# Two cached attention blocks on one core: every tile as two half-width loads, one per DMA queue

## The chip, the cores and the metric

The kernel runs on one core of a Trainium2 chip. The metric is the device time of one execution in microseconds, lower is better.

## The reference

Two independent decode blocks, A and B, have the same shapes: 8 sequences, one new token each, width 1024, 32 heads of 128, and a cache of 4096 keys and values. All inputs are bf16.

```python
# for each of A and B
q = (x @ wq).reshape(8, 1, 32, 128).transpose(0, 2, 1, 3)
scores = einsum("bhqd,bhkd->bhqk", q, k_cache) * 128 ** -0.5
p = softmax(scores)
o = einsum("bhqk,bhkd->bhqd", p, v_cache)
out = o.transpose(0, 2, 1, 3).reshape(8, 1, 4096) @ wo
# and the two results side by side along the last axis
```

The two caches of a block hold 2 x 268 MB; with the four projection matrices the kernel reads 1107 MB, and every byte of it once.

## The kernel before, in words

The work is cut into 64 iterations (`NQ`), each for one block, one sequence and 8 heads. An iteration n has one K tile and one V tile. A tile is 128 partitions x 64 KB = 8.39 MB: partition (head, m) holds 256 consecutive positions of the cache, 64 KB that are contiguous in HBM too. The projection matrices `wq` and `wo` of the two blocks are tiles of the same size, so there are 132 tiles in all.

SBUF has room for three tiles, the `ring`. In the steady state K tiles alternate between slots 0 and 1, and every V tile goes to slot 2. The order is written out by hand in `plan`:

```python
plan = [("wq", 0, 1), ("k", 0, 0), ("wq", 1, 2)]
for n in range(NQ - 1):
    plan.append(("k", n + 1, (n + 1) % 2))
    plan.append(("v", n, 2))
plan += [("v", NQ - 1, NQ % 2), ("wo", 0, 2), ("wo", 1, (NQ - 1) % 2)]
```

`load_tiles` (L257) goes down this list and issues a load as soon as the operation that last uses the slot's previous tenant has been written into the program (`opUse`); the load then waits on a semaphore for that operation. For V(n) this is the second half of PV of n-1 (L382), for K(n+2) it is the last reduction matmul group of n (L345). In the kernel before, V loads are issued by ScalarE on its own DMA queue, all other tiles by SyncE. Each ring slot has one semaphore, and each `dma` call adds 16 to the count that its readers wait for. Output rows go out on both queues, and the two small x inputs come in on ScalarE's.

The program is a list of operations per engine, written in one order; each engine executes its own list in that order. An iteration has four chunks r = 0..3 of a K tile:

- DVE multiplies the chunk by the broadcast query (L330, in place), folds its halves (L335), and one chunk later sums what PE has reduced (L353).
- PE reduces the folded chunk by matmuls with the identity (`make_eacc`, L345). At r = 2 the first half of PV of iteration n-1 stands ahead of that reduction on PE, and so does the broadcast of the next query (L317); at r = 3 the second half of PV does (L382). `make_ext` (L399) follows after the reduction of r = 3.
- At r = 0 the softmax of n-1 is done: maximum (L359), exp on ScalarE (L365), and the spread probabilities `PM` on DVE (L370).
- ScalarE copies PV's result (L390, `make_acc`), the extracted output (L405) and stages and copies the next query (L312, L319).

At r = 3 the order of the writing is PV's second half, `make_acc`, the reduction, `load_tiles`, `make_ext`. So `load_tiles` there issues V(n) and K(n+2), in this order. PE's and DVE's lists are folded into hardware loops of two iterations; ScalarE's and SyncE's are straight code. After the loop the last softmax, the normalization (L418, L419) and the output projections (L433) follow. The last `wo` is loaded in three pieces (`wo_cuts`), of 48, 12 and 4 KB in each partition.

Of the kernel before, what the change touches and what calls it, by code (L numbers as in the profile page):

```python
# [31 lines left out]
class _Program:  # L32
# [11 lines left out]
    def add(self, eng, emit, deps=(), dma_key=None, moves=False):  # L44
        op = _Op(eng, emit, list(deps), dma_key, moves)
        if dma_key is not None:
            self.counts[dma_key] = self.counts.get(dma_key, 0) + 16
            op.token = (dma_key, self.counts[dma_key])
        for d in op.deps:
            if not (d.eng == "pe" and eng == "pe"):  # L50
                d.sig = True
        self.ops[eng].append(op)
        return op
# [86 lines left out]
def _build_kernel(nc, caches, out):  # L140
    B, Sq, D = caches[0][0].shape
    _, H, Sk, Dh = caches[0][1].shape
    NC = len(caches)
    assert B == 8 and Sq == 1 and Dh == 128 and Sk == 4096 and D == 1024 and H % 8 == 0 and 128 % H == 0
    DC = D // 128
# [16 lines left out]
    with es:  # L162
# [45 lines left out]
        def dma(out_ap, in_ap, key, deps, eng="sp"):  # L208
            return add(eng, lambda e: e.dma_start(out_ap, in_ap), deps, dma_key=key)


        def pool_select(view, base, pattern, dep, op=ALU.not_equal, fill=1.0, step=1):
            return add("pool", lambda e: e.affine_select(out=view, in_=view, compare_op=op, fill=fill,
                                                         base=base, pattern=pattern, channel_multiplier=step), [dep])
        c_ident = pool_select(ident[:], 0, [[-1, 128]], add("pool", lambda e: e.memset(ident[:], 0.0)))


        c_own = add("pool", lambda e: e.memset(own_m[:], 1.0))
        c_own = pool_select(own_m[:], 0, [[-MP, HQ], [0, PH]], c_own, ALU.is_ge, 0.0)
        c_own = pool_select(own_m[:], MP - 1, [[MP, HQ], [0, PH]], c_own, ALU.is_ge, 0.0, -1)  # L220
        own = own_m[:, :, 0]

# [8 lines left out]
        opT, opMul, opEacc, opRed, opNgm, opExp = {}, {}, {}, {}, {}, {}  # L231
# [18 lines left out]
        def where(n):  # L250

            return n // (B * HB), n // HB % B, n % HB
# [4 lines left out]
        def load_tiles():  # L257
            while issued[0] < len(plan):
                kind, n, w = plan[issued[0]]
                prev = before[issued[0]]  # L260
                dep = opUse.get(prev)
                if prev is not None and dep is None:
                    return
                to, key = ring[:, w, :], ("t", w)
                if kind in ("k", "v"):
                    c, b, hb = where(n)
                    from_ = caches[c][1 if kind == "k" else 2][b, hb * HQ:(hb + 1) * HQ].rearrange("u (m t) d -> (u m) (t d)", m=MP)
                    opT[(kind, n)] = dma(to, from_, key, [dep], "act" if kind == "v" else "sp")
                elif kind == "wq":
                    opT[(kind, n)] = dma(to[:, 0:DC * H * Dh], caches[n][3].rearrange("(p k) n -> p (k n)", k=DC), key, [dep])  # L270
                else:
                    from_ = caches[n][4].rearrange("(p r) n -> p (r n)", r=H)
                    for i, (r0, r1) in enumerate(wo_cuts if n == NC - 1 else ((0, H),)):
                        opT[(kind, n, i)] = dma(to[:, r0 * D:r1 * D], from_[:, r0 * D:r1 * D], key if n < NC - 1 else ("w", i), [dep])
                issued[0] += 1


# [169 lines left out]
        def emit_xT(e):  # L447
# [5 lines left out]
            return i  # L453
        op_xT = opUse[("x", 0)] = add("pe", emit_xT, [c_ident, op_x[-1]])
        load_tiles()
        c_xT = add("dve", lambda e: e.tensor_copy(xT[:], misc_bf16[:, 0:NC * DC * B]), [op_xT])
        make_q(0)
# [5 lines left out]
        for n in range(NQ):  # L463
            P.mark(n)
            for r in range(NR):
                s = n * NR + r
                make_mul(s)
                if s >= LAG:
                    make_red(s - LAG)
                if r == LAG - 1 and n >= 1:  # L470
                    make_shift(n - 1)
                fold = make_fold(s)
                if r == LAG - 1 and n >= 1:
                    make_pm(n - 1)
                if n == 0 and r == 1:
                    for c in range(1, NC):
                        make_q(c)
                        make_qT(c)
                if r == 2 and n >= 1:
                    make_pv(n - 1, 0, RG // 2)  # L480
                if r == 3 and n >= 1:
                    make_pv(n - 1, RG // 2, RG)
                    make_acc(n - 1)
                if r == 2 and n + 1 < NQ:
                    make_stage(n + 1)
                    make_qbc(n + 1)
                make_eacc(s, fold)
                load_tiles()
                if r == 3 and n >= 1:
                    make_ext(n - 1)  # L490
        P.mark(NQ)
        n = NQ - 1
# [4 lines left out]
        make_pv(n, 0, RG)  # L497
        make_acc(n)
        load_tiles()
        make_ext(n)  # L500
        make_norm(1)
# [31 lines left out]
def bass_concat_heads__mha_block_cached__mha_block_cached__decode_kernel(  # L533
    nc, A_x, A_k_cache, A_v_cache, A_wq, A_wo, B_x, B_k_cache, B_v_cache, B_wq, B_wo, out,
):
    caches = [(A_x, A_k_cache, A_v_cache, A_wq, A_wo), (B_x, B_k_cache, B_v_cache, B_wq, B_wo)]
    _build_kernel(nc, caches, out)
# [28 lines left out]
```

## Time and profile before

| | |
|---|---|
| median of 3 runs | 2931.91 us (2924.83 to 2936.99) |
| the profiled execution's own time | 2936.99 us |
| its span | 2935.2 us |
| DMA, mean over the span | 377 GB/s, 1107.53 MB |
| share of the two load queues (q1 SyncE, q10 ScalarE) | 44.9% and 43.7% of 16 engines |
| DVE, PE, ScalarE busy | 74%, 39%, 4% |
| TensorE clock granted | 0.688 of full speed |

The span runs from the first to the last instruction of the profiled execution. "Busy" is the time of the instructions themselves. In the chain of waits each moment is put down to what held up the end; a DMA in it counts from its issue to its landing. The line numbers L... are those of the kernel before.

### The profile page before, as it was taken

What the parts mean: (1) busy time and instruction counts of PE and PEld (TensorE: products, weight loads), DVE (VectorE), ACT (ScalarE), POOL (GpSimd) and SP (SyncE); (2) the same over time, 40 slices, a digit from 0 to 9 for tenths busy, and PEclk for the clock granted to TensorE, in tenths of its full rate; (3) what the DMA queues carried; (4) which work ended last, traced back from release to release, by engine and by line L of the source; (5) the groups of instructions that cost most, each with busy time, mean ns of one, the idle gap of its engine ahead of it and who ended that gap; (6) DMA issues with size and microseconds to landing.
All of it is one profiled execution on the core that took longest, in us unless ns stands there. A gap on an engine that the chain in (4) does not pass through costs nothing.

```text
span 2935.2 us, 18256 instructions
## 1 busy us (share of the span) xinstructions
PE 1155.4 (39%) x7648; PEld 401.4 (14%) x7648; DVE 2172.8 (74%) x1043; ACT 130.0 (4%) x401; POOL 2.5 (0%) x14
## 2 busy tenths in 40 slices
PE   2433443443433334334334434333344344344344
PEld 1111111111111111111111111111111111111112
DVE  2977768778778678777777787786777877877864
ACT  1000000000000000000000000000000000000000
POOL 0000000000000000000000000000000000000000
PEclk7666766766667667767767666676676676676667
DMA  9989889889889898898898898898988988988989
GB/s 428 401 371 388 372 343 400 372 372 400 357 372 400 343 400 372 359 400 370 372 400 343 372 398 359 372 400 343 400 351 364 400 371 358 400 372 372 395 348 387
DMA packets 19436, 1107.53 MB, mean 377 GB/s; under 512 B 2208, under 2 KB 2256, under 8 KB 2400
## 3 DMA queue, kind: packets, MB, share of 16 engines
q1 hardware_dynamic: 10128, 570.45, 44.9%
q10 hardware_dynamic: 9296, 536.92, 43.7%
q8 instruction: 7, 0.11, 0.0%
q14 instruction: 5, 0.04, 0.0%
HBM read 1107.33 MB, written 0.03 MB: 377 GB/s over the span
## 4 chain that ended last, share of the span: by engine, by line
DMA 79%; PE 17%; DVE 3%; another core or an unknown queue 0%; issue 0%; ACT 0%; SPq 0%; DVEq 0%
DMA ring<-in_A_v_cache_dram 39%; DMA ring<-in_B_v_cache_dram 37%; PE pv L382 11%; PE red L345 5%; DVE ring L330 1%; DMA ring<-in_A_k_cache_dram 1%; DMA ring<-in_B_wo_dram 1%; DVE ring L335 1%; PE misc L317 0%; DVE s_sb L353 0%; PE proj L433 0%; DVE PM L370 0%; PE o L285 0%; PE pv L285 0%
## 5 line engine op out<-in xcount | busy, mean ns | idle before, releaser
L330 DVE TENSOR_TENSOR ring<-ring,qbc 128x8192 bf16<-128x8192 bf16 x256 | 1131.4, 4420 | 13.6 <-DMA ring<-in_A_k_cache_dram 13.6
L345 PE MATMUL red<-ring,ident 128*128 128x512 bf16 x2048 | 746.2, 530 | 927.0 <-DVE ring L335 927.0
L353 DVE TENSOR_REDUCE s_sb<-red 128x64 f32<-128x1024 f32 x256 | 312.2, 1220 | 659.8 <-PE red L345 659.8
L382 PE MATMUL pv<-ring,PM 128*32 128x512 bf16 x4096 | 349.5, 502 | 799.9 <-DMA ring<-in_A_v_cache_dram 400.1
L335 DVE TENSOR_TENSOR ring<-ring 128x4096 bf16<-128x4096 bf16 x256 | 582.2, 2274 | 0.0
L345 PEld LDWEIGHTS red<-ring,ident 128*128 128x128 bf16 x2048 | 237.1, 125 | 1357.8 <-DVE ring L335 1023.8
L382 PEld LDWEIGHTS pv<-ring,PM 128*32 128x32 bf16 x4096 | 118.9, 117 | 1026.4 <-DMA ring<-in_A_v_cache_dram 427.6
L370 DVE TENSOR_TENSOR PM<-pe,own_h 128x2048 bf16<-128x2048 bf16 x64 | 146.2, 2284 | 0.7 <-ACT pe L365 0.7
L319 ACT ACTIVATE qbc<-misc 128x128 bf16<-128x128 f32 x64 | 17.8, 277 | 1954.2 <-PE misc L317 1954.2
L390 ACT ACTIVATE accS<-pv 128x512 bf16<-128x512 f32 x64 | 38.2, 597 | 276.6 <-PE pv L382 276.6
L365 ACT ACTIVATE pe<-s_sb,ngm 128x256 bf16<-128x256 f32 x64 | 32.5, 508 | 257.4 <-DVE ngm L363 257.4
L399 PE MATMUL o<-accS,E 128*32 128x32 bf16 x1024 | 36.3, 177 | 0.7 <-ACT accS L390 0.7
L399 PEld LDWEIGHTS o<-accS,E 128*32 128x32 bf16 x1024 | 29.6, 94 | 28.7 <-issue 27.5
L359 DVE TENSOR_REDUCE rmax<-s_sb 128x1 f32<-128x256 f32 x64 | 26.9, 420 | 2.2
L305 DVE COPY qT<-misc 128x64 bf16<-128x64 bf16 x8 | 3.5, 435 | 33.2 <-PE misc L301 33.2
L405 ACT ACTIVATE o_sb<-o 32x32 f32<-32x32 f32 x64 | 11.9, 186 | 226.6 <-PE o L399 226.0
L433 PE MATMUL proj<-ring,on_sb 128*8 128x256 bf16 (+1 forms) x192 | 15.3, 413 | 12.6 <-DMA ring<-in_A_wo_dram 6.7
L438 DVE CAST orow<-proj 40x512 bf16<-40x512 f32 (+1 forms) x2 | 1.1, 554 | 25.6 <-PE proj L433 25.6
L312 ACT ACTIVATE qst<-qT 128x128 bf16<-128x128 bf16 x64 | 18.7, 293 | 2.0 <-DVE qT L305 1.9
L317 PE MATMUL misc<-ident,qst 128*128 128x128 bf16 x64 | 18.2, 284 | 0.9 <-ACT qst L312 0.9
L360 DVE TENSOR_SCALAR rtmp<-half,rmax 128x32 f32<-128x32 f32 x64 | 15.5, 241 | 2.3
L363 DVE TRANSPOSE_TENSOR_REDUCE ngm<-rtmp 128x1 f32<-128x32 f32 x64 | 13.5, 211 | 2.2
(33 smaller groups left out, 67.8 us busy)
## 6 DMA issues: line engine op xcount, KB each, us to landing
ring<-in_B_wo_dram SPq DMA_DIRECT2D x1, 6144.0 KB, 37.2
ring<-in_B_wo_dram SPq DMA_DIRECT2D x1, 1536.0 KB, 40.6
ring<-in_A_k_cache_dram SPq DMA_DIRECT2D x32, 37.6
ring<-in_A_v_cache_dram ACTq DMA_DIRECT2D x32, 36.3
ring<-in_B_k_cache_dram SPq DMA_DIRECT2D x32, 37.6
ring<-in_B_v_cache_dram ACTq DMA_DIRECT2D x32, 36.3
ring<-in_B_wo_dram SPq DMA_DIRECT2D x1, 512.0 KB, 40.1
out_dram<-orow SPq DMA_DIRECT2D x2, 4.0 KB
```

What stands on the lines that cost most here:

```text
L312: return e.activation(qst[:, n % 2, :].rearrange("p (j m) -> p j m", m=MP), from_.unsqueeze(2).to_broadcast([128, HQ, MP]), ACTF.Copy)
L317: opQb[n] = add("pe", lambda e: e.matmul(misc[:, 0:Dh], qst[:, n % 2, :], ident[:], start=True, stop=True), [opSt[n], _at(opQbc, n - 1), c ...
L330: opMul[s] = add("dve", lambda e: e.tensor_tensor(v, v, qbc[:, n % 2, :].unsqueeze(1).to_broadcast([128, CT, Dh]), ALU.mult), [opT[("k", n ...
L335: return add("dve", lambda e: e.tensor_tensor(v[:, :, 0:64], v[:, :, 0:64], v[:, :, 64:128], ALU.add), [opMul[s]])
L345: i = e.matmul(dst, ident[:], v[:, g, :, j, :], start=(j == 0), stop=(j == 3))
L353: opRed[s] = add("dve", lambda e: e.tensor_reduce(s_sb[:, n % 2, r * CT:(r + 1) * CT], red_ps[s % 2][:, :].rearrange("p (t w) -> p t w", w ...
L359: m = add("dve", lambda e: e.tensor_reduce(rmax[:], s_sb[:, n % 2, :], AX.X, ALU.max), [opRed[NR * n + NR - 1]])
L365: opExp[n] = add("act", lambda e, at: e.activation(pe[:], s_sb[:, n % 2, :], ACTF.Exp, bias=ngm[:, n % 2:n % 2 + 1], scale=scale, accum_ou ...
L370: opPM[n] = add("dve", lambda e: e.tensor_tensor(PM[:], pe[:].unsqueeze(2).to_broadcast([128, T, HQ]), own_h[:].unsqueeze(1).to_broadcast( ...
L382: i = e.matmul(pv_ps[32 * q:32 * (q + 1), :], PM[:, t:t + 4, :].rearrange("p t j -> p (t j)"), v[:, t * Dh:(t + 4) * Dh], start=(g == 0), ...
L390: opAcc[n] = add("act", lambda e: e.activation(accS[:], pv_ps[:], ACTF.Copy), [opPV[n], _at(opExt, n - 1)])
L399: x = e.matmul(to, E[:, i, PH - 1 - u:PH - 1 - u + MB], accS[:, i * 128 + H * u:i * 128 + H * (u + 1)], start=(i == 0 and u == 0), stop=(i ...
```

## The change

Every tile is loaded by two DMAs, each with half of the tile's columns, which is 32 KB of each partition's 64 KB. The left half is issued by SyncE on its queue, the right half by ScalarE on its queue. This holds for K, V, wq and every piece of wo. Both halves raise the same semaphore of the slot, so that readers wait for twice the count; the second half's operation is the one that readers depend on. The order of tiles, the slots, the operations that a load waits for, and the loops of PE and DVE stay as they are. ScalarE's program was straight code and is so after the change.

```diff
+        def tile_dma(out_ap, in_ap, key, deps):
+            cut = out_ap.shape[1] // 2
+            dma(out_ap[:, 0:cut], in_ap[:, 0:cut], key, deps)
+            return dma(out_ap[:, cut:], in_ap[:, cut:], key, deps, "act")
...
-                    opT[(kind, n)] = dma(to, from_, key, [dep], "act" if kind == "v" else "sp")
+                    opT[(kind, n)] = tile_dma(to, from_, key, [dep])
                 elif kind == "wq":
-                    opT[(kind, n)] = dma(to[:, 0:DC * H * Dh], caches[n][3].rearrange("(p k) n -> p (k n)", k=DC), key, [dep])
+                    opT[(kind, n)] = tile_dma(to[:, 0:DC * H * Dh], caches[n][3].rearrange("(p k) n -> p (k n)", k=DC), key, [dep])
                 else:
...
-                        opT[(kind, n, i)] = dma(to[:, r0 * D:r1 * D], from_[:, r0 * D:r1 * D], key if n < NC - 1 else ("w", i), [dep])
+                        opT[(kind, n, i)] = tile_dma(to[:, r0 * D:r1 * D], from_[:, r0 * D:r1 * D], key if n < NC - 1 else ("w", i), [dep])
```

## The prediction

> **What bounds the kernel now.** I read the page's head and its chain first, then the waits, then one iteration of the steady state, then the end of the kernel, where one iteration runs under other conditions.
>
> ```profile
> PE 1155.4 (39%) x7648; PEld 401.4 (14%) x7648; DVE 2172.8 (74%) x1043; ACT 130.0 (4%) x401; POOL 2.5 (0%) x14
> DMA packets 19436, 1107.53 MB, mean 377 GB/s; under 512 B 2208, under 2 KB 2256, under 8 KB 2400
> DMA ring<-in_A_v_cache_dram 39%; DMA ring<-in_B_v_cache_dram 37%; PE pv L382 11%; PE red L345 5%; DVE ring L330 1%; DMA ring<-in_A_k_cache_dram 1%; DMA ring<-in_B_wo_dram 1%; DVE ring L335 1%; PE misc L317 0%; DVE s_sb L353 0%; PE proj L433 0%; DVE PM L370 0%; PE o L285 0%; PE pv L285 0%
> ```
>
> No engine is full. The chain is made of V loads (76%) and PV (11%); K loads have 1% of it. So it is not plain DMA bandwidth that ends last: it is the loop "V loads, PV reads it, the next V may load". The waits say the same:
>
> ```profile
> DVE s_sb L353 <- PE red L345: 659.8, 62, 13.6
> PE pv L382 <- DMA ring<-in_A_v_cache_dram: 400.1, 31, 15.5
> PE pv L382 <- DMA ring<-in_B_v_cache_dram: 399.8, 31, 15.5
> DVE ring L330 <- DMA ring<-in_A_k_cache_dram: 13.6, 2, 10.2
> ```
>
> PE waits 12 to 15 us for V in each of 61 iterations (799.9 us), and DVE then waits behind PE (659.8 us), since the first half of PV stands ahead of the next reduction matmuls on PE. K costs DVE only 13.6 us, at the start. The chain of one iteration, and DMA over it (window, its length, five engines' busy us with counts, clock, DMA share, GB/s):
>
> ```profile
> 1016.28 36.28 DMA ring<-in_A_v_cache_dram
> 1052.61 3.61 PE pv L382 x32
> 1056.21 0.22 PE misc L317
> 1056.43 2.52 PE red L345 x8
> 1058.96 1.87 PE pv L382 x32
> ...
> 1060.86 36.38 DMA ring<-in_A_v_cache_dram
> ```
> ```profile
> 1016.28:1060.86 44.58, 17.78 (x113) 6.07 (x113) 33.82 (x17) 1.86 (x7) 0.00 (x0) 0.66 0.89 376
> ```
>
> The period is 36.3 us of V load plus 8.3 us of PE; over the 60 iterations from V issue 164.54 to V issue 2849.47 it is 44.75 us. DMA is busy 0.89 of it: 39.7 us of work, and a hole of about 5 us. DVE has 33.8 us of work. The V load is slow because K is issued 3.55 us after it (SyncE, 1019.83) on the other queue, and both then share the engines: V lands after 36.3 us, K after 37.6, and both 8.39 MB tiles together need 41.1 us from V's issue. V is needed at once, K only an iteration later; the sharing gives K half of the rate just when only V is urgent.
>
> The end of the kernel shows what happens without that sharing. From 2849.47 no K remains; two V tiles are issued back to back on ScalarE's queue, then wo:
>
> ```profile
> 2849.47 3.89 ACTq L209 DMA_DIRECT2D ring<-in_B_v_cache_dram  x2
> 2881.04 0.60 ACT L390 ACTIVATE accS<-pv 128x512 bf16<-128x512 f32 x1 [22.93 <-PE pv L382]
> ```
> ```profile
> 2849.47:2911.26 61.79, 25.40 (x232) 9.84 (x232) 42.58 (x26) 3.55 (x10) 0.00 (x0) 0.72 1.00 430
> 22.80:62.87 40.07, 10.89 (x105) 4.11 (x106) 16.12 (x9) 5.29 (x10) 0.00 (x0) 0.68 0.97 419
> ```
>
> The first of these V tiles has all the bandwidth, PV does not wait, and PV to PV is 31.6 us in place of 44.6; DMA is at share 1.00 for three tiles (V 62, V 63, wo 0). The second window is k 0 and the second wq, back to back on one queue: 40.07 us for two tiles.
>
> **What the Trainium skill says.** *DMA: Bandwidth & Descriptors*, Queues, rings and completion order: a copy is spread over up to 16 engines, each takes its queue's descriptors in order and goes round-robin between queues. The trace agrees: V at 36.3 and K at 37.6 us are what half a rate each gives, and V 63 behind V 62 on one queue did not slow V 62. The same page, Issuing engines are not separate DMA queues: two issuing engines save only issue time. Agreed: share 1.00 with one queue (419 to 430 GB/s). So the two queues bring no bandwidth; what they bring or lose is order. The same page, Bandwidth: 425 GB/s for a large load alone; measured here 419 to 430.
>
> **The change, part by part.**
>
> *Order (the large one).* Each tile becomes two halves, one per queue, and both queues get V(n) first, then K(n+2): SyncE and ScalarE both issue in plan order, V(n) on PV(n-1), K(n+2) on the last Eacc of n, which PE does after it. So K no longer shares with V, it stands behind it. Take K(n+1) landed at 0 and DVE starting n+1. From the undisturbed last iteration (its first multiply at 2850.95): Eacc of chunk 1 ends at 2873.1, +22.1; PV ends at 2881.0, +30.1; the last Eacc ends at 2888.5, +37.6. V(n), already queued, lands at about +19.8, ahead of +22.1: the 12.7 us wait for V goes to about nothing. V(n+1) is issued at +30.1, while K(n+2) runs to +39.6: 9.5 us to spare. K(n+3) is issued at +37.6, while V(n+1) will run to +59.4. Both queues always hold work, and the hole of 5 us closes. DVE ends at about +33.9 and waits some 6 us for K(n+2). What is late next is K: the period is the DMA time of two tiles.
>
> *That time.* 16.78 MB: 39.7 us (0.89 x 44.58 us), 40.07 (the window at the start), 39.0 (16.78 MB at 430 GB/s). I take 19.8 us a tile.
>
> *Sum.* Start to 62.87 us is DMA-bound before and after (wq, k 0, wq are three tiles back to back): same. There remain 129 tiles (64 K, 64 V and 4 of projections, less these three) x 19.8 = 2554.2 us, so the last bytes land at 2617.1. Before, they land at 2930.7 (last piece of wo 1 issued at 2890.6, 40.1 us to landing); from there to the end of the span 4.5 us (2935.2 - 2930.7), and 1.8 us outside it (2936.99 - 2935.2). So 62.9 + 2554.2 + 4.5 + 1.8 = 2623 us for an execution like the profiled one, 314 less than its 2936.99. That execution is the slowest of the three shown, the median is 5 us lower; I take part of that and forecast 2620.
>
> *Rows of 32 KB, not 64.* Twice as many pieces. The trace has no such tile. Nearest: the last tile, cut into rows of 48, 12 and 4 KB, landed whole by 2930.7, 19.4 us after wo 0 at 2911.26: no loss to be seen. Gain: none, since the share was already 1.00. Loss: between 0 and 1 us a tile (129 us in all); I take 0.
>
> *More issues.* SyncE goes from 70 load issues to 134, ScalarE from 64 to 134 (out and x apart), 0.33 us each. ScalarE: 70 x 0.33 = 23 us beside an engine that is 4% busy. Its K issue waits for the last Eacc, and behind it stand the o copy (L405), then exp and the query staging. The o copy waits for ext, which PE does after that same Eacc (ACT at 1020.33, Eacc ended about 1019.8), and exp waits for a DVE reduction still later (1024.3). So cost 0; with that cover gone, 64 x 0.33 = 21 us (one issue, behind two others on SyncE's queue at 2888.91, took 1.64 us; even that ends before exp is due). SyncE's K issue stands behind its V issue, whose PV is earlier on PE: 0. GpSimd has no loads.
>
> *Waits.* A tile still has one semaphore, now raised by both halves; the reader waits for 32 in place of 16. No wait instruction is added for DVE or PE. It needs the later half: both queues are filled within some 0.3 us, so 0 to 2.5 us (one 32 KB row at half rate, an estimate from 19.8 us for eight 64 KB rows an engine), hidden where the stream is continuous. The tail is alike: wo 0 and wo 1 are issued 9.5 and 20 us or more before the queue runs dry.
>
> **The rivals.**
>
> *A, slower: half rows cost throughput.* Two queues reading the same tile 32 KB apart, twice the pieces. It decides when a tile needs more than (2937 - 69.2) / 129 = 22.2 us, 2.4 us over mine, or 0.15 us for each of 16 half rows on an engine. At 23.5 us a tile (357 GB/s) the kernel takes 129 x 23.5 + 69.2 = 3101. For it: nothing in the trace shows 32 KB rows on both queues. Against: K and V on both queues together ran at about 429 GB/s (16.78 MB in 41.1 us less some 2 us of latency), and small wo rows lost nothing.
>
> *B, DMA gains but not fully:* skew between the queues, so that K of one queue runs while V of the other is not finished, at 20.8 us a tile (k 0 landed 20.8 us after the first wq): 129 x 20.8 + 69.2 = 2752.
>
> *C, the change doesn't change the order:* one queue gets far ahead, V again takes 36 us, period 44.7: 2930. Against: V and K shared evenly before, and both queues now have equal lists.
>
> *D, DVE or PE becomes the bound:* 34 us of DVE is 6 below the DMA period; only if red and PV collide anew by more than that.
>
> **How the numbers follow.** Main case 0.72, with 19.4 to 20.4 us a tile: 2572 to 2701. B (and D) 0.14, to 2790. C 0.04. A 0.10, of which a few in 100 only just slower. Range 2555 to 2775: 19.3 us a tile less the median's 5 us at the lower end, B at the upper. Faster by over 0.5% (about what a measurement of this kernel can tell from no change): 0.87; within: 0.03; slower: 0.10.
>
> **What would show it.** Right: DMA share 9 in all slices and 415 to 430 GB/s; the two queues near 554 MB each; PE's wait for V from 800 to under 100 us; DVE waiting for K (L330) some 300 to 400 us; DVE's wait at L353 gone; K landing some 42 us after its issue, V some 29; the chain turning from V and PV to a mix of loads. DVE busy unchanged near 2173 us. Wrong: GB/s below 380 with a share of 9 (A); PV still waiting 12 us with K and V landing together (C); idle DMA with no wait for K (D).

## The result, and the profile after

The changed kernel takes 2581.18 us (median of 3 runs, 2581.08 to 2583.24) against 2931.91 us before: a ratio of 0.881, 95% interval 0.878 to 0.884. The forecast was 2620 us and faster.

The page of the changed kernel: PE's busy line, DMA, and the chain by line. Its lines 335, 340, 350, 358, 387 are 330, 335, 345, 353, 382 of the kernel before.

```profile
PE 1123.6 (44%) x7648; PEld 395.1 (15%) x7648; DVE 2172.7 (84%) x1043; ACT 129.9 (5%) x401; POOL 2.5 (0%) x14
DMA packets 38733, 1107.54 MB, mean 429 GB/s; under 512 B 4352, under 2 KB 4400, under 8 KB 4928
q1 hardware_dynamic: 19344, 553.67, 49.9%
q10 hardware_dynamic: 19376, 553.71, 49.9%
...
DMA ring<-in_B_k_cache_dram 25%; DMA ring<-in_A_k_cache_dram 25%; DVE ring L335 10%; DVE ring L340 10%; PE red L350 4%; DVE s_sb L358 4%; DVE PM L375 3%; DMA ring<-in_B_wo_dram 1%; DVE rmax L364 1%; DVE rtmp L365 0%; PE proj L438 0%; ACT PM L296 0%; PE o L290 0%; DVEq L135 0%
```

DVE has the same work as before (2172.7 us), the bytes are the same, and DMA now moves them at 429 GB/s instead of 377, with half on each queue. The V loads, 76% of the chain before, are gone from it; K loads stand there, with the DVE work between a K's landing and the next K's issue.

The waits of the changed kernel (us in total, times, longest):

```profile
DVE ring L335 <- DMA ring<-in_B_k_cache_dram: 159.3, 32, 5.6
DVE ring L335 <- DMA ring<-in_A_k_cache_dram: 152.4, 30, 8.9
...
PE pv L387 <- DVE PM L375: 4.7, 1, 4.7
DVE s_sb L358 <- PE red L350: 3.4, 1, 3.4
```

PE's 799.9 us of waiting for V no longer appear, and with them went DVE's 659.8 us behind PE. DVE waits 311.7 us for K in their place.

One iteration of the changed kernel: DVE's first multiply with its wait, SyncE's two issues, PE's first half of PV; then DMA over the steady state (window, length, five engines, clock, share, GB/s).

```profile
1019.84 4.42 DVE L335 TENSOR_TENSOR ring<-ring,qbc 128x8192 bf16<-128x8192 bf16 x1 [4.97 <-DMA ring<-in_A_k_cache_dram]
1058.67 4.43 DVE L335 TENSOR_TENSOR ring<-ring,qbc 128x8192 bf16<-128x8192 bf16 x1 [4.92 <-DMA ring<-in_A_k_cache_dram]
```
```profile
1049.92 0.33 SPq L209 DMA_DIRECT2D ring<-in_A_v_cache_dram  x1
1057.07 0.33 SPq L209 DMA_DIRECT2D ring<-in_A_k_cache_dram  x1
```
```profile
1041.99 2.33 PE L387 MATMUL pv<-ring,PM 128*32 128x512 bf16 x32
```
```profile
400.00:2400.00 2000.00, 871.62 (x5772) 303.88 (x5773) 1741.24 (x827) 95.60 (x309) 0.00 (x0) 0.68 1.00 432
```

The period is 38.8 us (1019.84 to 1058.67). PV starts 22.2 us after DVE's start on K, with no wait for V in its line; V(n+1) is issued at +30.1 and K(n+3) at +37.2. At both points DMA still has work, so its share is 1.00.

### The profile page after: what moved, and what is told of

Same layout as the page of the kernel before. It is cut to its first block, busy times and chain, and to the rows that moved or that the text cites. A ratio compares the mean times of both kernels' runs of the same rounds, so it can differ in the third digit from the quotient of the medians.

```text
span 2579.3 us, 18390 instructions
## 1 busy us (share of the span) xinstructions
PE 1123.6 (44%) x7648; PEld 395.1 (15%) x7648; DVE 2172.7 (84%) x1043; ACT 129.9 (5%) x401; POOL 2.5 (0%) x14
## 4 chain that ended last, share of the span: by engine, by line
DMA 52%; DVE 28%; issue 16%; PE 5%; another core or an unknown queue 0%; ACT 0%; DVEq 0%; ACTq 0%
DMA ring<-in_B_k_cache_dram 25%; DMA ring<-in_A_k_cache_dram 25%; DVE ring L335 10%; DVE ring L340 10%; PE red L350 4%; DVE s_sb L358 4%; DVE PM L375 3%; DMA ring<-in_B_wo_dram 1%; DVE rmax L364 1%; DVE rtmp L365 0%; PE proj L438 0%; ACT PM L296 0%; PE o L290 0%; DVEq L135 0%
## 5 line engine op out<-in xcount | busy, mean ns | idle before, releaser
L350 PE MATMUL red<-ring,ident 128*128 128x512 bf16 x2048 | 781.9, 551 | 1391.7 <-DVE ring L340 1391.7
L387 PE MATMUL pv<-ring,PM 128*32 128x512 bf16 x4096 | 275.0, 416 | 4.7 <-DVE PM L375 4.7
L387 PEld LDWEIGHTS pv<-ring,PM 128*32 128x32 bf16 x4096 | 104.2, 104 | 189.1 <-issue 117.4
L290 PE MATMUL o<-ring,xT 128*8 128x512 bf16 x64 | 7.2, 627 | 27.7 <-DMA ring<-in_A_wq_dram 18.3
## 6 DMA issues: line engine op xcount, KB each, us to landing
ring<-in_A_k_cache_dram ACTq DMA_DIRECT2D x32, 4096.0 KB, 40.2
ring<-in_A_v_cache_dram ACTq DMA_DIRECT2D x32, 4096.0 KB, 28.1
ring<-in_B_k_cache_dram ACTq DMA_DIRECT2D x32, 4096.0 KB, 40.2
ring<-in_B_v_cache_dram ACTq DMA_DIRECT2D x32, 4096.0 KB, 28.1
```

The costliest lines, as they stand in the source:

```text
L350: i = e.matmul(dst, ident[:], v[:, g, :, j, :], start=(j == 0), stop=(j == 3))
L387: i = e.matmul(pv_ps[32 * q:32 * (q + 1), :], PM[:, t:t + 4, :].rearrange("p t j -> p (t j)"), v[:, t * Dh:(t + 4) * Dh], start=(g == 0), ...
```

## The experiments

The theory, "order": V was late because K took half of the rate; with V(n) ahead of K(n+2) in one line, V comes in time and DMA never runs dry. Its rivals: two queues on one tile bring bandwidth ("parallel queues"), or 32 KB rows move better than 64 KB rows ("shorter rows").

**One queue, whole tiles (e1_one_queue).** Order kept, halves and second queue taken away.

```diff
         def tile_dma(out_ap, in_ap, key, deps):
-            cut = out_ap.shape[1] // 2
-            dma(out_ap[:, 0:cut], in_ap[:, 0:cut], key, deps)
-            return dma(out_ap[:, cut:], in_ap[:, cut:], key, deps, "act")
+            return dma(out_ap, in_ap, key, deps)
```

> The changed kernel's order of tiles, but every tile whole (64 KB rows) and all on SyncE's queue; ScalarE issues only x and half of the outputs. Theory 'order' (V(n) stands in front of K(n+2) in one line, so the queue is never empty and V has the whole rate): DMA share 1.00, about 430 GB/s, period 39 us, 2570 to 2600 us, like the changed kernel. Rival 'parallel queues' (two queues on one tile bring the bandwidth): DMA stays near 0.9 share or 380 to 420 GB/s, 2650 us or more. Rival 'shorter rows': 64 KB rows again, so near 2930 us.

Measured: 2566.54 us, ratio to the kernel before 0.872 (0.869 to 0.875), 3.5 us below the range of "order". Its DMA queues (packets, MB, share) and steady state:

```profile
q1 hardware_dynamic: 19344, 1107.32, 99.8%
q10 hardware_dynamic: 80, 0.05, 0.0%
```
```profile
400.00:2400.00 2000.00, 880.25 (x5852) 307.09 (x5852) 1750.51 (x830) 96.85 (x311) 0.00 (x0) 0.68 1.00 434
```

One queue with 64 KB rows carries 434 GB/s at share 1.00, a little more than two. Both rivals fall: neither the second queue nor the shorter rows is needed for any of the gain.

**Halves, but on the old queues (e2_halves_own_queue).** Shorter rows kept, order taken away.

```diff
-        def tile_dma(out_ap, in_ap, key, deps):
+        def tile_dma(out_ap, in_ap, key, deps, eng="sp"):
             cut = out_ap.shape[1] // 2
-            dma(out_ap[:, 0:cut], in_ap[:, 0:cut], key, deps)
-            return dma(out_ap[:, cut:], in_ap[:, cut:], key, deps, "act")
+            dma(out_ap[:, 0:cut], in_ap[:, 0:cut], key, deps, eng)
+            return dma(out_ap[:, cut:], in_ap[:, cut:], key, deps, eng)
...
-                    opT[(kind, n)] = tile_dma(to, from_, key, [dep])
+                    opT[(kind, n)] = tile_dma(to, from_, key, [dep], "act" if kind == "v" else "sp")
```

> Every tile in two halves as in the changed kernel, but both halves on one queue: V's on ScalarE's, all others on SyncE's, as before. Theory 'order': V and K share the rate again, V lands some 36 us after its issue, PE waits about 800 us for V, period 44.7 us: 2915 to 2945 us. Rival 'shorter rows': most of the gain stays, 2580 to 2650 us.

Measured: 2915.2 us, ratio 0.990 (0.987 to 0.993). Its waits are those of the kernel before:

```profile
DVE s_sb L358 <- PE red L350: 639.9, 62, 13.4
...
PE pv L387 <- DMA ring<-in_A_v_cache_dram: 391.4, 31, 15.2
PE pv L387 <- DMA ring<-in_B_v_cache_dram: 389.2, 31, 13.2
```

As "order" expected, at the lower edge of its range. The 1% that halves bring here is small beside the change's 12%; its cause was not followed up.

**K in front of V (e3_k_first).** Queues, halves and bytes of the changed kernel, the list turned round.

```diff
-        plan = [("wq", 0, 1), ("k", 0, 0), ("wq", 1, 2)]
+        plan = [("wq", 0, 1), ("k", 0, 0), ("wq", 1, 2), ("k", 1, 1)]
         for n in range(NQ - 1):
-            plan.append(("k", n + 1, (n + 1) % 2))
+            if n + 2 < NQ:
+                plan.append(("k", n + 2, n % 2))
             plan.append(("v", n, 2))
```

> The changed kernel with the list of tiles turned round: K(n+2) is put in front of V(n) on both queues; the same bytes, halves and queues. Theory 'order': V(n) is issued only at the end of n's last reduction and lands two tiles later, about 40.5 us; from there to the next such point 11.9 us (1052.6 to 1064.4 in the trace of the kernel before), so a period of about 52 us and 3300 to 3450 us in all, with DMA idle a quarter of the time. Rivals 'parallel queues' and 'shorter rows': two queues and 32 KB rows are kept, so near 2580 us.

Measured: 3460.63 us, ratio 1.175 (1.171 to 1.179). Its chain over one iteration, with V's load at both ends:

```profile
995.47 41.16 DMA ring<-in_A_v_cache_dram
1036.67 3.60 PE pv L388 x32
...
1046.60 1.91 PE red L351 x8
...
1048.54 0.36 ACTq L209
1048.93 41.02 DMA ring<-in_A_v_cache_dram
```

V lands 41 us after its issue, about the time of two tiles. The period is 53.5 us here and 52.9 on average (estimate 52), and the total is 10 us above the expected range. Of the 8.9 us that this iteration is longer than that of the kernel before (44.6), 4.9 are V's longer load. The other 4.0 are its later issue: V stands behind K(n+2) in both lines, so it too waits for the last reduction. DMA is at share 0.75 from 1000 to 2000 us. The order of two loads alone moves this kernel between 2581 and 3461 us.

**K held until V has landed (e4_hold_k).** The kernel before, whole tiles on their own queues, with one wait more on SyncE.

```diff
-                    opT[(kind, n)] = dma(to, from_, key, [dep], "act" if kind == "v" else "sp")
+                    held = [opT[("v", n - 2)]] if kind == "k" and n >= 2 else []
+                    opT[(kind, n)] = dma(to, from_, key, [dep] + held, "act" if kind == "v" else "sp")
```

> The kernel before (whole tiles, V on ScalarE's queue, K on SyncE's) with one more wait: K(n+2) is not issued until V(n) has landed. Theory 'order' in its narrow form (K's sharing of the rate is what makes V late): V lands some 21 to 23 us after its issue, PE no longer waits for V, K still lands in time: 2570 to 2680 us, at the upper end if each hand-over from V to K leaves DMA idle for some 2 us. If instead the single line without gaps is what matters, or the sharing was not the cause: 2750 us or more.

Measured: 2744.26 us, ratio 0.933 (0.929 to 0.936), outside the expected range, and just short of the 2750 us given for the other answer. PE's line for PV, the waits of DVE for K, and two windows of DMA: the steady state, and 5 us around a hand-over (V landed and K was issued at 1059.15):

```profile
L383 PE MATMUL pv<-ring,PM 128*32 128x512 bf16 x4096 | 277.1, 418 | 4.6 <-DVE PM L371 4.6
```
```profile
DVE ring L331 <- DMA ring<-in_A_k_cache_dram: 238.0, 28, 18.1
DVE ring L331 <- DMA ring<-in_B_k_cache_dram: 235.2, 32, 10.0
```
```profile
400.00:2400.00 2000.00, 827.00 (x5506) 288.00 (x5505) 1635.14 (x774) 90.44 (x290) 0.00 (x0) 0.67 0.95 406
...
1058.00:1063.00 5.00, 1.94 (x5) 0.74 (x6) 5.00 (x3) 0.00 (x0) 0.00 (x0) 0.50 0.60 210
```

PE's wait for V is gone, so the sharing was what made V late. V lands a median 26.8 to 27.9 us after its issue, not the 21 to 23 expected: it is issued while K is still coming in (at 1033.35, K landed at 1042.31), and shares with K's end. And DMA is at 0.95: holding K puts an idle stretch of 2 us (0.4 of the second window) between V's last bytes and K's first, 5% of a period of 41.3 us (16.78 MB at 406 GB/s). In the trace's packet records, which have start and length of every packet, it is 1.9 us on average over 50 hand-overs; the changed kernel has no such stretch. So "order" has two parts: V ahead of K is worth about 200 us (2944 to 2744), and no gap between them a large part of the remaining 178 us (1.9 us x 64 = 124, an estimate).

**K held for 7/8 of V (e7_hold_k_for_7_8).** This tests the gap: V comes as 7/8 and 1/8 on ScalarE's queue, and K waits for the first only. The last eighth counts on semaphores of its own, and PV waits for both.

```diff
-                    opT[(kind, n)] = dma(to, from_, key, [dep], "act" if kind == "v" else "sp")
+                    held = [opV[n - 2]] if kind == "k" and n >= 2 else []
+                    cut = T * Dh * 7 // 8
+                    if kind == "v":
+                        opV[n] = dma(to[:, 0:cut], from_[:, 0:cut], key, [dep], "act")
+                        opT[(kind, n)] = dma(to[:, cut:], from_[:, cut:], ("r", n // (NQ - 1)), [dep], "act")
+                    else:
+                        opT[(kind, n)] = dma(to, from_, key, [dep] + held)
...
```

> As the run in which K(n+2) was held until V(n) had landed (2744 us), but V comes in two pieces of 7/8 and 1/8, and K waits only for the first; the last 1/8 (1 MB, 2.4 us at full rate) keeps DMA busy while K's load starts. If the loss of that run against one line (2744 - 2566 = 178 us, 2.8 us an iteration) is the idle hand-over of about 2 us from V to K: 2590 to 2640 us, DMA share 0.99 or more. If it is that V and K still share the rate for part of the time: 2710 to 2760 us again.

Measured: 2642.41 us, ratio 0.900 (0.897 to 0.902), 2 us above the expected range, and with a DMA share just below the 0.99 expected:

```profile
400.00:2400.00 2000.00, 851.82 (x5626) 296.12 (x5630) 1686.96 (x799) 92.42 (x299) 0.00 (x0) 0.67 0.98 418
```

102 of the 178 us come back, so the gap is real and the larger part of that run's loss. In the packet records the idle time at a hand-over falls from 1.9 to 0.7 us on average and not to nothing: at the one at 1062.5 us the last eighth is almost over when K is issued (DMA is down to a share of 0.2). The period is 40.1 us (16.78 MB at 418 GB/s), 1.4 us above that of one line at 434 GB/s. The 0.6 us that are left beside the idle time (0.7 in e4) were not settled.

**Where the changed kernel loses 15 us to one queue.** Three runs, measured together on one chip: the changed kernel again (after_again), both halves on SyncE's queue (e6_halves_one_queue), and eighths on alternating queues (e5_eighths).

```diff
# e6
-            return dma(out_ap[:, cut:], in_ap[:, cut:], key, deps, "act")
+            return dma(out_ap[:, cut:], in_ap[:, cut:], key, deps)
# e5
+            cut = out_ap.shape[1] // 8
+            for i in range(8):
+                last = dma(out_ap[:, i * cut:(i + 1) * cut], in_ap[:, i * cut:(i + 1) * cut], key, deps, "act" if i % 2 else "sp")
+            return last
```

> The changed kernel once more, as the measure for the other runs of this group on the same chip: 2575 to 2590 us.

> The changed kernel with both halves of every tile on SyncE's queue: 32 KB rows, one queue. It splits the 14.6 us between the changed kernel (2581) and whole tiles on one queue (2566.5). If the second queue costs them (ScalarE's half starts behind x and lands later than SyncE's): 2564 to 2570 us. If the shorter rows cost them: 2577 to 2585 us.

> Every tile in eight loads of an eighth of its columns (8 KB rows), alternating between the two queues. If a row has a price that explains the 14.6 us (1056 more rows an engine, so 14 ns each), then 48 more rows an engine and tile cost 48 x 132 x 14 ns = 89 us: about 2670 us, and the DMA rate falls to some 415 GB/s at share 1.00. If rows of this size are free: 2575 to 2590 us, GB/s as in the changed kernel. Eight issues a tile on two engines (4 x 0.35 us) should cost nothing either way.

Measured: 2580.93, 2576.61 and 2651.15 us (ratios 0.878, 0.877 and 0.902). DMA in the steady state of halves on one queue and of eighths on two:

```profile
400.00:2400.00 2000.00, 878.47 (x5807) 306.18 (x5811) 1742.35 (x826) 95.60 (x309) 0.00 (x0) 0.68 1.00 432
```
```profile
400.00:2400.00 2000.00, 856.31 (x5674) 297.67 (x5674) 1693.74 (x801) 93.20 (x301) 0.00 (x0) 0.67 1.01 422
```

Halves on one queue lie between the two expectations, 0.4 us below the second: both causes have a part. The second queue costs 4.3 us (2580.93 - 2576.61). That leaves the shorter rows 10.9 of the 15.2 us between the changed kernel and one queue with whole tiles (measured side by side below).

The rows' part is a price in the steady state. From the landing of K 10 to that of K 60 an iteration takes 38.71 us with whole tiles on one queue, 38.87 with halves on one queue, 38.89 in the changed kernel and 39.82 with eighths. Halves are 16 more rows an engine and iteration, eighths 96 more than halves: 10 ns a row in both steps. More rows are also more loads here, but the packet records tell the two apart. From 400 to 2400 us a row of 64 KB takes an engine 2422 ns (e1), one of 32 KB 1217 (e6) and one of 8 KB 314 (e5), some 12 ns for each further row into which 64 KB are cut; the write that reports a load's end takes 9 ns, once a load.

Over 64 iterations this makes 60 of the 70.2 us that eighths cost. The other 10 lie at the end, so the expectation that the issues cost nothing fails there: ScalarE's nine issues of the last wo take 30.8 us, and the last softmax stands behind them. From the last landing to the end of the span it is 14.5 us, in after_again 3.7.

The second queue's part lies mostly at the start; a window of the changed kernel, and the same of whole tiles on one queue:

```profile
118.00:126.00 8.00, 3.76 (x41) 1.50 (x42) 8.00 (x5) 0.60 (x1) 0.00 (x0) 0.92 0.45 160
```
```profile
118.00:126.00 8.00, 4.07 (x24) 1.23 (x16) 8.00 (x4) 0.60 (x1) 0.00 (x0) 0.80 0.99 393
```

PE begins with the first wq at 27.7 us on two queues and 22.9 us on one. ScalarE's half is issued 0.95 us later, behind x. In the packet records of the first 8 us its queue moves 0.3 MB and SyncE's 2.4; SyncE's then goes on to k 0 while ScalarE's still brings wq, and the two halves of each of the first four tiles end 6 to 7 us apart. Everything after starts some 3.5 us later (V 1 is issued at 122.1 instead of 118.6; with halves on one queue it is 118.6 too), and here, once, DMA runs dry for about 4 us.

**The two side by side (e8_one_queue_again, e9_after_beside).** The kernels of e1 and of the change once more, together on one chip.

> Whole tiles, all on SyncE's queue, once more beside the changed kernel on one chip, since the two were measured in different groups: 2564 to 2570 us, 0.4 to 0.7% below the changed kernel, with intervals that don't touch. If the difference was the chip's: within 0.2% of it.

> The changed kernel beside the one-queue version on one chip: 2578 to 2585 us.

Measured: 2566.67 us (2566.18 to 2567.71) and 2581.86 us (2580.44 to 2582.43). Whole tiles on one queue beat the changed kernel by 15.2 us, 0.6%, and the kernel before by 12.8% (ratio 0.872, 0.869 to 0.875). It is the fastest version found.

## Why the prediction was right, point by point

- **Bound before, a loop of V's load and PV, not bandwidth:** right (PE's waits for V were 62, of 9 to 15.5 us, not 61 of 12 to 15). Halves on the old queues leave it (2915 us), turning the list lengthens it by V's longer load and later issue (3461 us), and holding K removes PE's wait for V (2744 us).
- **Order, and what is late next:** right, to within 0.4 us in the iteration shown. PV at +22.1 forecast, +22.2 measured; V issue +30.1 and +30.1; K issue +37.6 and +37.2 (in the next iteration +35.9). DVE waits 311.7 us for K, forecast 300 to 400. K has landed with both halves a median 40.2 us after its issue, V 28.1 (42 and 29 forecast). The chain has K's loads and none of V's, where a mix of loads was forecast.
- **Time of a tile, 19.8 us:** this is the term that was mis-sized. From the second wq (66.4 us) to the last landing (2575.5 us) a tile takes 19.45 us, and 129 tiles x 0.35 us are 45 us, more than the whole error of 39 us; the later start below gives 3.5 of them back. The step that failed is reading 0.89 x 44.58 us = 39.7 us as DMA's work: at the 432 to 434 GB/s of a full line the same 16.78 MB take 38.7 to 38.8 us, so the share overstates the work of that window by 2%. The 40.07 us of the window at the start were too long as well, with DMA at 0.97 there. The third of its figures, 39.0 us from the full line at the kernel's end, was the best of them.
- **Start unchanged at 62.9 us:** wrong by 3.5 us: the second wq is there at 66.4 us, since SyncE's queue runs ahead of ScalarE's at the start and a tile is complete only with its later half.
- **Rows of 32 KB at no cost:** wrong in size, not in range: about 11 us in all where 0 was taken and up to 129 allowed. It is part of the 19.45 us.
- **More issues, and ScalarE's K issue ahead of the o copy:** right. In the changed kernel the K issue at 1057.08 ends before the o copy may start at 1057.58, as PE's ext ends only then; ScalarE is 5% busy.
- **Both halves within 0.3 us of issue, so alike:** right in the steady state: issued at 1049.92 and 1049.93, and in the packet records of 400 to 2400 us the last packets of the two halves are less than 0.01 us apart (forecast 0 to 2.5). Wrong for the first four tiles, with 6 to 7 us.
- **Rival A (half rows cost throughput):** its mechanism exists, at 10 ns for each of the 8 more rows an engine and tile, where 0.3 us each (the prediction's 0.15 us for each of 16 half rows) were needed to turn the sign. Even eighths stay 288 us below the kernel before (2651.15 against 2939.33 in that group). B's skew between the queues occurred at the start alone, where it cost some 3.5 us. C and D did not occur: V comes in time, and DVE's wait behind PE's reduction is 3.4 us.

What the Trainium skill (*DMA: Bandwidth & Descriptors*, Issuing engines are not separate DMA queues) says, that loads from several engines interleave on the same DMA engines and save only issue time, is what e1 and e6 show: the second queue brought no bandwidth and cost 4.3 us.

## What to carry to other kernels

Where two streams of loads share the DMA engines, look at which one is needed first: on two queues they shared the rate here (V and K landed after 36.3 and 37.6 us), and the urgent one was late by what the other took. Put both into one line in the order of need, with the next load issued before the line runs dry; holding the second back by a semaphore cost an idle hand-over each time (1.9 us here). Then use as few queues and as long rows as the tile allows; here the two were worth 4 and 11 us.

## What the runs showed of the hardware

A contiguous row of 8 KB in place of 32 KB lowered a full DMA line from 432 to 422 GB/s, about 10 ns a row and engine; 64 KB rows gave 434. The same page's Specifications give 512 B as the minimum for line rate; here rows sixteen times that long still lose 2 to 3% against long ones. A load issued only when another had landed left DMA idle for 1.9 us on average (e4); a load already queued left nothing idle in the packet records.
